# Three more groups convolved as split float32r parts, their row loads moved, and a pass's last products reordered

## The chip, the cores and the metric

The kernel runs on one core of a Trainium2 chip. The core has five engines that run their own instruction streams in order: TensorE (PE, matrix products; its weight loads are listed as PEld), VectorE (DVE), ScalarE (ACT), GpSimd (POOL) and SyncE (SP), which here issues most transfers. The metric is the device time of one execution in microseconds (us); lower is better. The kernel before takes 1276.77 us, the median of three runs (1275.79 to 1277.69).

## The reference

The input x has 8 sequences of 3584 rows of 192 float32 values. A causal convolution with 7 taps, one softmaxed tap vector for each of 8 heads of 24 columns, is followed by a routed two-layer network: each of the 28672 rows goes to the one of 8 experts with the highest gate logit.

```python
w = softmax(weight)                                   # (8 heads, 7 taps)
out = einsum('hk,bskhg->bshg', w, windows of x_pad)   # x -> (28672, 192)
logits = x @ w_gate + modality_bias[modality_id]
e_idx = argmax(logits); gate_w = softmax(logits)[e_idx]
for e in range(8):
    h = maximum(x[mask] @ w1[e], 0.0)                 # 192 -> 1024
    out[mask] = gate_w[mask, None] * (h @ w2[e])      # 1024 -> 192
```

## The kernel before

**Routing.** The rows are taken in 19 groups (`QUADS_OF_GROUP`), of up to 16 tiles of 112 rows; a quad is 4 tiles, 384 KB of x. For a group the kernel loads its quads (`load`), convolves the 8 heads (`convolve`), turns the result (`turn`, DVE transposes), computes gate logits on PE (`gate`), picks the expert (`choose`), computes each row's place in its expert's list (`place`) and scatters rows and gate weight to the DRAM buffer `routed_rows` from POOL (`send`).

**Two ways to convolve.** The groups below `WHOLE_X` multiply the float32 rows (tile `x`) with the float32 matrix `band`, one matmul for each head, which the profile shows as two records. The others first split the rows into a float32r high part `xh` (a cast on ACT, L100) and the rest `xl` (a subtraction on DVE, L101), and add three float32r products: `xh`·`band_hi`, `xl`·`band_hi`, `xh`·`band_lo`. Their quads arrive in a ring of three buffers `xr`, of which the first, `xr_0`, is also the memory of `band`; the first load into it must wait for the last float32 convolution.

**Experts.** Whenever enough rows are routed, a table (`table`) hands out slots: an expert and a number of passes of 256 rows. A slot loads its expert's weights (`Slot.__init__`, into `raw`), gathers its rows from `routed_rows` (`bring`, tiles `near`, `far`, `tags`), splits the weights into float32r parts (`Slot.split`: `w1b`, `w2b`, again a cast on ACT and a subtraction on DVE), and turns the rows of each pass (`turn`: `tp`, `sxh`, `sxl`, `sxs`). A pass has four steps. In a step, `first` makes ten products (L704) of the rows with w1 into `hps`, ACT makes `hh` (relu) and DVE makes `hl` (L708) from it; two steps later `second` multiplies `hh` and `hl` with `w2b` into two PSUM tiles `po`, one for each half of the pass's rows. After a pass's last step `put` scales `po` on ACT (`lowp`) and DVE (`o`, L740), and POOL scatters it to the output.

**Order.** The routing of later groups is cut into parts, and `run` advances as many parts in each step as `due` says, from marks that count the parts of the groups (`parts_of`). ACT keeps the order of the program; on the other engines a scheduler sets it. Every engine then executes its own list in order.

```python
QUADS_OF_GROUP = (1, 1, 2, 2, 2) + (4,) * 14
WHOLE_X = 10
LAG = 2
GROUPS_OF_CHUNK = (5, 2, 2, 2, 2, 2, 2, 2, 0, 0)
SLOTS_OF_CHUNK = (4, 3, 3, 4, 3, 4, 3, 3, 3)
PASSES_OF_SLOT = (2, 4, 4, 4, 4, 4, 4, 4, 2, 1)
```

So the first 4 slots have 2 passes each, 32 steps, during which the rest of groups 5 and 6 and most of group 7 are routed; later slots have 4 passes.

Of the kernel before, what the change touches and what calls it, by code (L numbers as in the profile page):

```python
# [18 lines left out]
P = 128  # L19
MB = 112  # L20
HALO = 16
QUADS_OF_GROUP = (1, 1, 2, 2, 2) + (4,) * 14
WHOLE_X = 10
WHOLE_Y = 5
HEAD_BANKS = dict(turn=1, logit=2, place=2)
ORDERED = {mybir.EngineType.Activation}
# [17 lines left out]
def conv_then_routed_ffn(ctx, tc, x, weight, modality, w_gate, mod_bias, w1, w2, out):  # L44
    nc = tc.nc
    NB, S, D = x.shape
# [8 lines left out]
    NF = FF // P  # L55
    NJ = T // P
# [27 lines left out]
    def ring(pool, n, shape, dtype, name, tag=None):  # L84

        tag = tag or name
        k = turns[tag] = turns.get(tag, -1) + 1
        return pool.tile(shape, dtype, name=name, tag=f"{tag}_{k % n}", bufs=1)
# [135 lines left out]
    class Group:  # L224


        def __init__(self, g, chunk):
            self.chunk, self.xr, self.whole_x, self.whole_y = chunk, [], g < WHOLE_X, g < WHOLE_Y
            self.place_x = ("xh", "xl")[g % 2 if self.whole_x else 0]
# [170 lines left out]
    def parts_of(g):  # L400

        return H + 5 + 3 * QUADS_OF_GROUP[g] + (QUADS_OF_GROUP[g + 1] if WHOLE_X <= g + 1 < NG else 0)

# [7 lines left out]

    def body(cur, after):

        if after:
            for q in range(min(3, after.quads)):
                after.load(q)
        for h in range(H):
            cur.convolve(h)
            yield
        cur.bias_of()  # L420
        gates = []
        ready, step_of = [], 1 if cur.whole_y else 2
        for t in range(cur.quads + 2):
            if t < cur.quads:
                cur.turn(t)
                yield
            if t == 0 and after and after.whole_x and after.quads > 3:
                after.load(3)
            if ready and ready[0][1] < t:
                t0, _, terms = ready.pop(0)  # L430
                gates.append((t0, cur.gate(terms)))
            yield
            if t < cur.quads:
                terms = cur.part_turned(t)
                if (t + 1) % step_of == 0 or t + 1 == cur.quads:
                    ready.append((4 * (t // step_of * step_of), t, terms))
            yield
            while gates:
                cur.logits(*gates.pop(0))
        cur.choose()  # L440
        yield
        if after and not after.whole_x:
            for q in range(after.quads):
                after.part(q)
                if q == 0 and after.quads > 3:
                    after.load(3)
                yield
# [163 lines left out]
    class Slot:  # L611


        def __init__(self, i, chunk, ent):
            self.i, self.h, self.passes, self.rows, self.ends, self.tags = i, {}, plan[chunk][2] // T, {}, {}, {}
            self.chunk, self.ent, load = chunk, ent, nc.sync
            with tc.issue_after(state["load"]) if "load" in state else nullcontext():
                e = load.value_load(ent[:, 1:2], min_val=0, max_val=E - 1)
                new = load.value_load(ent[:, 2:3], min_val=0, max_val=1)
            w1e = w1[bass.ds(e, 1), :, :].rearrange("e p n -> (e p) n")  # L620
            w2e = w2[bass.ds(e, 1), :, :].rearrange("e (c p) d -> p (e c) d", p=P)
            only = dict(cond=new, cond_hint=False)
            load.dma_start(out=raw1[i % 2][:, 0, :], in_=w1e[0:P, :], **only)
            for r in range(2):
                state["load"] = load.dma_start(out=raw1[i % 2][r * DB:(r + 1) * DB, 1, :], in_=w1e[P:D, :], **only).ins

            def load_second():
                state["load"] = load.dma_start(out=raw2[i % 2], in_=w2e, **only).ins

            self.load_second = load_second  # L630
            if i > 0:
                load_second()
# [78 lines left out]
        def second(self, k, fp):  # L711
            wb = w2b[self.i % 2]
            hh, hl = self.h.pop((k, fp))
            if fp == 0:
                self.po = [ring(ps_g2, 2, [P, 2 * D], F32, "po") for _ in range(NJ)]
            for u in range(2):
                c = 2 * fp + u
                for j, po in enumerate(self.po):
                    js = slice(j * P, (j + 1) * P)

                    def by_hi():
                        nc.tensor.matmul(po, hh[:, u, js], wb[:, c, :], start=c == 0, stop=c == NF - 1,  # L722
                                         skip_group_check=True)

                    def by_lo():
                        nc.tensor.matmul(po[:, 0:D], hl[:, u, js], wb[:, c, 0:D], start=False, stop=False,  # L726
                                         skip_group_check=True)

                    for product in (by_lo, by_hi) if c == NF - 1 else (by_hi, by_lo):
                        product()  # L730
            if fp == NF // 2 - 1:
                self.put(self.h.pop(("tag", k)))

# [201 lines left out]
```

## Time and profile before

| | us |
|---|---|
| median of three runs | 1276.77 |
| the profiled execution | 1274.14 |
| its span, first to last instruction | 1272.4 |
| PE busy / PEld busy | 1221.3 / 1187.7 |
| DVE busy | 1001.7 |
| ACT busy | 736.9 |
| POOL busy | 519.2 |

The profiled execution is one run of its own: 1.74 us lie around its span, and it stands 2.63 us below the median. Busy time counts an engine's instructions once where they overlap. A row of a window gives its length, then for each engine the busy time and in brackets the number of instructions, then the TensorE clock that was granted, the share of time in which the DMA engines were busy, and GB/s.

### The profile page before, as it was taken

Reading aid. Unit: us, or ns where it says so; the run is one execution under the profiler, and the core shown is the slowest. Engines: PE = TensorE matmul, PEld = TensorE weight load, DVE = VectorE, ACT = ScalarE, POOL = GpSimd, SP = SyncE. Lnnn points to the kernel's source line nnn. Section 1 sums busy time; section 2 is a strip of 40 time slices with the busy share of each in tenths; the row PEclk is TensorE's granted clock in tenths of the full one; section 3 lists DMA queues with packets and bytes.
Section 4 is the critical chain, followed back from the end, with each engine's and each line's share of the span. In section 5 each row is a group of like instructions: output and inputs, shape, how many; then the busy total and the mean of one; then the engine's idle time right before and its main releaser. Section 6 shows DMA issues by size and latency. Waiting matters only on the chain.

```text
span 1272.4 us, 28546 instructions
## 1 busy us (share of the span) xinstructions
PE 1221.3 (96%) x9106; PEld 1187.7 (93%) x9106; DVE 1001.7 (79%) x2545; ACT 736.9 (58%) x1644; POOL 519.2 (41%) x574
## 2 busy tenths in 40 slices
PE   8559999999999999999999999999999999999996
PEld 6438899999999999999999999999999999999996
DVE  6559988887888778877888788877876676687895
ACT  2226565566666556656665666556555555566774
POOL 5745763625353532624454442613526122121221
PEclk9869999999999999999999999999999999999999
DMA  6567475435453445424355445424424135494440
GB/s 180 158 164 174 125 196 106 108 83 134 100 145 79 98 95 120 133 44 111 63 133 147 110 103 119 114 56 103 101 48 132 37 77 109 104 248 105 91 101 18
DMA packets 314836, 142.24 MB, mean 112 GB/s; under 512 B 229042, under 2 KB 301355, under 8 KB 314676
## 3 DMA queue, kind: packets, MB, share of 16 engines
q1 hardware_dynamic: 289060, 94.97, 35.4%
q0 software_dynamic: 23232, 44.30, 11.0%
q8 instruction: 73, 1.20, 0.4%
q10 hardware_dynamic: 2384, 1.06, 0.3%
q14 instruction: 87, 0.71, 0.2%
HBM read 118.16 MB, written 51.82 MB: 134 GB/s over the span
## 4 chain that ended last, share of the span: by engine, by line
PE 77%; DVE 7%; issue 4%; DMA 4%; POOL 3%; SPq 2%; ACT 2%; DVEq 0%; POOLq 0%; ACTq 0%
PE hps L704 36%; PE po L722 23%; PE po L726 11%; PE cv L276 5%; PE gt L320 3%; POOL routed_rows L212 2%; DVE hl L708 2%; SPq L653 2%; DVE w1b L101 1%; DMA raw<-in_moe_w_dram 1%; DMA routed_rows<-y,idx 1%; DVE w2b L101 1%; DMA near<-routed_rows 1%; ACT lowp L738 0%; DVE sxs L691 0%
## 5 line engine op out<-in xcount | busy, mean ns | idle before, releaser
L722 PE MATMUL po<-w2b,hh 128*128 128x384 f32 x1824 | 556.2, 355 | 3.6 <-DVE o L740 3.4
L704 PE MATMUL hps<-sxh,w1b 128*128 128x256 f32 x1824 | 484.7, 288 | 2.7 <-DVE hl L708 1.3
L741 POOL DMA_INDIRECT out_dram<-o,tags x228 | 233.6, 1024 | 555.8 <-DVE o L740 492.2
L707 ACT ACTIVATE hh<-hps 128x512 fp32r<-128x512 f32 x456 | 273.1, 599 | 314.4 <-PE hps L704 309.1
L708 DVE SCALAR_TENSOR_TENSOR hl<-hps,hh 128x512 fp32r<-128x512 f32 x456 | 311.2, 685 | 178.0 <-ACT hh L707 175.5
L726 PE MATMUL po<-w2b,hl 128*128 128x192 f32 x1824 | 442.6, 253 | 0.0
L704 PE MATMUL hps<-sxs,w1b 128*128 128x256 f32 x1824 | 363.3, 281 | 0.5 <-DVE sxs L691 0.5
L704 PEld LDWEIGHTS hps<-sxh,w1b 128*128 128x128 f32 x1824 | 343.9, 189 | 12.7 <-DVE hl L708 7.9
L722 PEld LDWEIGHTS po<-w2b,hh 128*128 128x128 f32 x1824 | 344.1, 189 | 5.4 <-DVE o L740 4.8
L726 PEld LDWEIGHTS po<-w2b,hl 128*128 128x128 f32 x1824 | 345.7, 190 | 0.0
L212 POOL DMA_INDIRECT routed_rows<-y,idx x256 | 253.7, 991 | 145.4 <-issue 114.2
L704 PEld LDWEIGHTS hps<-sxs,w1b 128*128 128x128 f32 x1824 | 279.6, 189 | 0.9 <-DVE sxs L691 0.7
L704 PE MATMUL hps<-sxl,w1b 128*128 128x256 f32 x912 | 256.1, 281 | 0.6 <-DVE sxl L691 0.6
L704 PEld LDWEIGHTS hps<-sxl,w1b 128*128 128x128 f32 x912 | 172.5, 189 | 3.2 <-DVE sxl L691 0.8
L101 DVE TENSOR_TENSOR w1b<-raw,w1b 128x512 fp32r<-128x512 f32 x152 | 101.1, 675 | 6.6 <-ACT w1b L100 6.1
L738 ACT ACTIVATE lowp<-po,tags 128x192 f32<-128x192 f32 x228 | 83.7, 418 | 31.8 <-PE po L722 31.3
L281 ACT COPY y<-cv 112x192 f32<-112x192 f32 (+1 forms) x198 | 53.4, 319 | 75.5 <-PE cv L276 54.6
L100 ACT CAST w1b<-raw 128x512 fp32r<-128x512 f32 x152 | 92.4, 620 | 0.8
L101 DVE TENSOR_TENSOR w2b<-raw,w2b 128x384 fp32r<-128x384 f32 x152 | 80.9, 542 | 10.3 <-ACT w2b L100 10.0
L740 DVE SCALAR_TENSOR_TENSOR o<-po,tags,lowp 128x192 f32<-128x192 f32 x228 | 84.9, 411 | 4.8 <-ACT lowp L738 2.5
L689 ACT CAST sxs<-tp 64x128 fp32r<-64x128 f32 x228 | 67.9, 298 | 32.6 <-DVE tp L682 29.8
L100 ACT CAST w2b<-raw 128x384 fp32r<-128x384 f32 x152 | 76.1, 512 | 1.0
(133 smaller groups left out, 1032.0 us busy)
## 6 DMA issues: line engine op xcount, KB each, us to landing
raw<-in_moe_w_dram SPq DMA_DIRECT2D x38, 768.0 KB
raw<-in_moe_w_dram SPq DMA_DIRECT2D x38, 512.0 KB
raw<-in_moe_w_dram SPq DMA_DIRECT2D x76, 256.0 KB
xr<-in_x_dram SPq DMA_DIRECT2D x36, 384.0 KB
near<-routed_rows SPq DMA_DIRECT2D x212, 64.0 KB
x<-in_x_dram SPq DMA_DIRECT2D x26, 384.0 KB
far<-routed_rows SPq DMA_DIRECT2D x456, 16.0 KB
routed_rows<-filler SPq DMA_DIRECT2D x8, 776.0 KB
```

The costliest lines, as they stand in the source:

```text
L100: nc.scalar.copy(out=hi, in_=raw)
L101: return nc.vector.tensor_tensor(out=lo, in0=raw, in1=f(hi), op=ALU.subtract).ins
L212: state["scatter"] = nc.gpsimd.indirect_dma_start(out=scr, out_offset=bass.IndirectOffsetOnAxis(ap=idx, axis=0), in_=src, in_offset=None,).ins
L689: nc.scalar.copy(out=hi, in_=raw)
L704: nc.tensor.matmul(hps[:, u, :], wa[:, c, fs], mv[z], start=n == 0, stop=n == len(terms) - 1)
L707: nc.scalar.activation(out=hh, in_=hps, func=AF.Relu)
L708: turn_behind(nc.vector.scalar_tensor_tensor(out=hl, in0=hps, scalar=0.0, in1=f(hh), op0=ALU.max, op1=ALU.subtract))
L722: nc.tensor.matmul(po, hh[:, u, js], wb[:, c, :], start=c == 0, stop=c == NF - 1, skip_group_check=True)
L726: nc.tensor.matmul(po[:, 0:D], hl[:, u, js], wb[:, c, 0:D], start=False, stop=False, skip_group_check=True)
L738: nc.scalar.activation(out=lowp, in_=po[:, D:2 * D], func=AF.Copy, scale=gate)
L740: turn_behind(nc.vector.scalar_tensor_tensor(out=o, in0=po[:, 0:D], scalar=gate, in1=lowp, op0=ALU.mult, op1=ALU.add))
L741: st = nc.gpsimd.indirect_dma_start(out=out, out_offset=bass.IndirectOffsetOnAxis(ap=tag.bitcast(I32)[:, j, 1:2], axis=0), in_=o, in_offse ...
```

## The change

It has four edits. `WHOLE_X` goes from 10 to 7, so groups 7, 8 and 9 are convolved by parts; with it `parts_of` counts four more parts for groups 6, 7 and 8, and `due` asks for them. In `body`, a group that is the first by parts has its first three quads loaded behind the convolution of the group ahead of it, not in front. The weight loads of slots 0 and 1 lose their condition. In `second`, the eight products of a pass's last step, for each half of a `u` pair, are sorted by half: all four of the first `po`, then all four of the second.

```diff
-WHOLE_X = 10
+WHOLE_X = 7
...
     def body(cur, after):
 
-        if after:
+        band_free = after and cur.whole_x and not after.whole_x
+        if after and not band_free:
             for q in range(min(3, after.quads)):
                 after.load(q)
         for h in range(H):
             cur.convolve(h)
             yield
+        if band_free:
+            for q in range(min(3, after.quads)):
+                after.load(q)
         cur.bias_of()
...
-            only = dict(cond=new, cond_hint=False)
+            only = dict(cond=new, cond_hint=False) if i > 1 else {}
...
-            for u in range(2):
-                c = 2 * fp + u
-                for j, po in enumerate(self.po):
-                    js = slice(j * P, (j + 1) * P)
...
+            at = [(u, j) for u in range(2) for j in range(NJ)]
+            if fp == NF // 2 - 1:
+                at = sorted(at, key=lambda uj: uj[1])
+            for u, j in at:
+                c, po = 2 * fp + u, self.po[j]
+                js = slice(j * P, (j + 1) * P)
...
```

What the change moves is seen in the instruction lists; the numbers behind names tell buffers apart, and lines 704, 708, 722, 726 and 740 of before are 708, 712, 728, 732 and 746 of after.

On DVE, before, behind the tenth `hl` stand the end of `choose` for group 6, the two `o` of a pass, and the next pass's `tp`:

```order
L708 SCALAR_TENSOR_TENSOR hl_1516<-hps_1504,hh_1515 128x512
L352 TENSOR_REDUCE first_1554<-rk_1551 112x16
L353 TENSOR_TENSOR oh_1550<-rk_1551,first_1554 112x128
L740 SCALAR_TENSOR_TENSOR o_1529<-po_1348,tags_841,lowp_1527 128x192
L740 SCALAR_TENSOR_TENSOR o_1536<-po_1349,tags_841,lowp_1534 128x192
L355 TENSOR_REDUCE den_1557<-ex_1547 112x16
L680 STREAM_TRANSPOSE tp_1566<-near_1074 128x256
L356 TENSOR_SCALAR den_1557<-den_1557 112x16
L101 TENSOR_TENSOR w1b0_89<-raw1_0_85,w1b0_89 128x512
```

The same place on DVE after the change, around the tenth `hl` and the two `o` of that pass:

```order
L101 TENSOR_TENSOR xl_1480<-xr_1204,xh_1479 128x768
L101 TENSOR_TENSOR w1b0_89<-raw1_0_85,w1b0_89 128x512
L712 SCALAR_TENSOR_TENSOR hl_1546<-hps_1534,hh_1545 128x512
L746 SCALAR_TENSOR_TENSOR o_1559<-po_1371,tags_841,lowp_1557 128x192
L746 SCALAR_TENSOR_TENSOR o_1566<-po_1372,tags_841,lowp_1564 128x192
L101 TENSOR_TENSOR xl_1480<-xr_1206,xh_1479 128x768
L101 TENSOR_TENSOR xl_1480<-xr_1208,xh_1479 128x768
L684 STREAM_TRANSPOSE tp_1579<-near_1070 128x256
L686 STREAM_TRANSPOSE tp_1579<-far_1071 128x128
L101 TENSOR_TENSOR xl_1480<-xr_1483,xh_1479 128x768
```

The four subtractions `xl` of group 7 now stand among these. Between the 4th and the 24th `hl` of the program DVE's list has 177 instructions before and 184 after: eight `xl` more (groups 7 and 8), one `idx` less, and otherwise the same.

On SP, before, three loads of group 7 (`x_968`) stand behind slot 0's second weight load, ahead of all that slot 1 asks for:

```order
L653 ISA
L653 DMA tags_841<-routed_rows 128x4x2
L628 ISA
L628 DMA raw2_0_87<-in_moe_w2_dram 128x8x192
L254 DMA x_968<-in_x_dram 128x4x192 x3
```

After, slot 1's table entry is read there at once, and group 7's loads stand later; its last quad, `xr_1483`, stands inside the gather of slot 3's rows:

```order
L632 DMA raw2_1_88<-in_moe_w2_dram 128x8x192
L643 TENSOR_LOAD tab_798
L643 ISA x2
L657 ISA
L657 DMA near_1516<-routed_rows 32x16x32
L254 DMA xr_1483<-in_x_dram 128x4x192
L657 ISA
L657 DMA near_1516<-routed_rows 32x16x32
```

On PE, before, the last step of a pass takes the two `po` in turn:

```order
L722 MATMUL po_7070<-w2b0_91,hh_7095 128x384
L726 MATMUL po_7070<-w2b0_91,hl_7096 128x192
L722 MATMUL po_7071<-w2b0_91,hh_7095 128x384
L726 MATMUL po_7071<-w2b0_91,hl_7096 128x192
L726 MATMUL po_7070<-w2b0_91,hl_7096 128x192
L722 MATMUL po_7070<-w2b0_91,hh_7095 128x384
L726 MATMUL po_7071<-w2b0_91,hl_7096 128x192
L722 MATMUL po_7071<-w2b0_91,hh_7095 128x384
```

After, it finishes one and then the other (here in another pass):

```order
L708 MATMUL hps_6763<-sxs_6663,w1b1_90 128x256 x2
L728 MATMUL po_6685<-w2b1_764,hh_6712 128x384
L732 MATMUL po_6685<-w2b1_764,hl_6713 128x192 x2
L728 MATMUL po_6685<-w2b1_764,hh_6712 128x384
L728 MATMUL po_6686<-w2b1_764,hh_6712 128x384
L732 MATMUL po_6686<-w2b1_764,hl_6713 128x192 x2
L728 MATMUL po_6686<-w2b1_764,hh_6712 128x384
```

The first `po` is complete four products ahead of the end where it was two ahead. The count and the kinds of products stay as they were.

More of the change, by code (lines that the diff above doesn't have):

```diff
@@ L715, in second, with by_hi, by_lo @@
                 self.po = [ring(ps_g2, 2, [P, 2 * D], F32, "po") for _ in range(NJ)]
-            for u in range(2):
-                c = 2 * fp + u
-                for j, po in enumerate(self.po):
-                    js = slice(j * P, (j + 1) * P)
[L721 to L730, printed above, removed]
+            at = [(u, j) for u in range(2) for j in range(NJ)]
[4 more added lines that the diff above has]
+                js = slice(j * P, (j + 1) * P)
+                def by_hi():
+                    nc.tensor.matmul(po, hh[:, u, js], wb[:, c, :], start=c == 0, stop=c == NF - 1,
+                                     skip_group_check=True)
+                def by_lo():
+                    nc.tensor.matmul(po[:, 0:D], hl[:, u, js], wb[:, c, 0:D], start=False, stop=False,
+                                     skip_group_check=True)
+                for product in (by_lo, by_hi) if c == NF - 1 else (by_hi, by_lo):
+                    product()
             if fp == NF // 2 - 1:
```

## The prediction

> **What bounds the kernel now.** I read the page's shares first, then the busy time by stretch, then the waits of the two busiest engines inside the stretch that the change touches.
>
> ```profile
> span 1272.4 us, 28546 instructions
> PE 1221.3 (96%) x9106; PEld 1187.7 (93%) x9106; DVE 1001.7 (79%) x2545; ACT 736.9 (58%) x1644; POOL 519.2 (41%) x574
> ```
>
> By these shares PE is the bound, and any product that the change saves would be time saved. But the shares are a mean over stages. I cut the span at the end of the 4th and of the 24th `hl` (steps 4 and 24), where the instruction lists begin and cease to differ most:
>
> ```profile
> 100.58 0.65 DVE L708 SCALAR_TENSOR_TENSOR hl<-hps,hh 128x512 fp32r<-128x512 f32 x1
> 168.42 0.68 DVE L708 SCALAR_TENSOR_TENSOR hl<-hps,hh 128x512 fp32r<-128x512 f32 x1
> ...
> 101.20:169.10 67.90, 62.33 (x433) 56.65 (x432) 64.19 (x178) 41.40 (x97) 39.41 (x41) 1.00 0.60 149
> 169.10:265.70 96.60, 96.40 (x710) 92.13 (x709) 79.77 (x200) 57.61 (x131) 51.26 (x56) 1.00 0.54 128
> 265.70:1180.00 914.30, 912.62 (x6993) 908.46 (x6993) 725.62 (x1777) 547.36 (x1198) 350.38 (x375) 1.00 0.46 105
> ```
>
> Behind 169 us PE is busy all the time (96.40 of 96.60) and DVE has a fifth of its time free. In the stretch from 101.2 to 169.1 us it is the other way: DVE is busy for 64.19 of 67.90 us, 94.5%, and PE stands for 5.6. Twenty steps take 67.90 us there, 3.4 each; behind it the next 36 (to the 60th `hl`) take 96.60, 2.7 each. The stretch is slow because weights are split for slots of only two passes while two and a half groups are routed. Who waits for whom in it:
>
> ```profile
> PE po L722 <- DVE o L740: 2.4, 3, 0.9
> PE gt L320 <- DVE gx L101: 1.5, 2, 1.2
> PE gt L320 <- ACT gx L100: 1.2, 1, 1.2
> PE hps L704 <- DVE hl L708: 0.2, 1, 0.2
> ...
> DVE w2b L101 <- ACT w2b L100: 0.9, 2, 0.6
> DVE w1b L101 <- ACT w1b L100: 0.8, 1, 0.8
> DVE hl L708 <- ACT hh L707: 0.6, 2, 0.3
> DVE o L740 <- ACT y L281: 0.2, 1, 0.2
> ```
>
> The upper rows are PE's, the lower DVE's, of this stretch alone. All but one of PE's waits end with a DVE instruction, and that one with the cast that feeds one. DVE's own waits come to 2.5 us and none is for a transfer. So DVE sets the time for twenty steps, and PE sets it from there to the last slots.
>
> [...]
>
> **DVE's added work.** Eight of the twelve new `xl` subtractions, those of groups 7 and 8, stand between the 4th and the 24th `hl` in the new list, and nothing else is added there. Their price:
>
> ```profile
> L101 DVE TENSOR_TENSOR xl<-xr,xh 128x768 fp32r<-128x768 f32 x36 | 33.9, 941 | 0.2
> 115.14 0.95 DVE L101 TENSOR_TENSOR gx<-turned,gx 128x768 fp32r<-128x768 f32 x1
> 116.01 1.02 DVE L101 TENSOR_TENSOR w2b<-raw,w2b 128x384 fp32r<-128x384 f32 x2
> ```
>
> One lasts 941 ns; back to back, the next instruction begins 0.87 us behind an operation of the same shape (115.14 to 116.01). I take 0.87: 8 × 0.87 = 7.0 us. If the added work filled all of DVE's free time in the stretch (67.90 − 64.19 = 3.7), the stretch would grow by 3.3; if the free time stayed, by 7.0. It can grow by more: between the tenth `hl` and the next the new list has three `xl`, 2.6 us more in one interval, and five heads of products follow in one piece on PE with four PSUM buffers, so PE and DVE wait for each other by turns. I allow 2 us for this, the size of PE's waits for `o` above. Between 3.3 and 9.0 I take 6.0: DVE's free time now comes in pieces behind ACT's casts, which do not get shorter, so about 1 us of it can be filled.
>
> [...]
>
> **ACT's added work.** The same eight casts are 0.83 us each, 6.6 us by the row below, on an engine that is busy for 41.40 of 67.90. I cost them at nothing: ACT's free 26.5 us hide them. Where they stand ahead of a relu they delay it by up to 0.83 us; that is in the 2 us above.
>
> ```profile
> L100 ACT CAST xh<-xr x36: 821/832/841, 281.2 to 866.3; 128x768 fp32r<-128x768 f32 x36
> ```
>
> **PE's products.** A float32 head costs 1.29/2 = 0.645 us; one by parts three starts 0.17 us apart, 0.52:
>
> ```profile
> 123.86 1.29 PE cv L276 x4
> ...
> 289.81 0.36 PE L722 MATMUL po<-w2b,hh 128*128 128x384 f32 x1
> 290.00 0.25 PE L726 MATMUL po<-w2b,hl 128*128 128x192 f32 x1
> 290.09 0.36 PE L722 MATMUL po<-w2b,hh 128*128 128x384 f32 x1
> 290.29 0.33 PE L276 MATMUL cv<-xh,band_hi 128*112 128x384 f32 x1
> 290.46 0.33 PE L276 MATMUL cv<-xl,band_hi 128*112 128x384 f32 x1
> 290.63 0.34 PE L276 MATMUL cv<-xh,band_lo 128*112 128x384 f32 x1
> 290.81 0.34 PE L276 MATMUL cv<-xh,band_hi 128*112 128x384 f32 x1
> ```
>
> That saves 0.125 us a head, 3.0 for 24. Eleven of the heads (group 7, three of group 8) lie in the stretch where PE waits anyway and save nothing. The 13 others lie behind it: −1.6 us. Group 9's four `xl` lie there too, beside PE, where DVE has 16.8 us free.
>
> **A pass's end.** The first `po` is complete 0.28 us earlier, one product of 384 columns and one of 192 (289.81 to 290.09 above). PE's waits for `o` are the only ones that this can shorten. The two behind 169 us come to 1.0 us by the row below, so the gain is between 0 and 2 × 0.28; I take −0.4. The three in the stretch are DVE's time and stay.
>
> ```profile
> PE po L722 <- DVE o L740: 1.0, 2, 0.8
> ```
>
> The order of products itself (one pair more of two narrow ones in a row, one of two wide) changes no count; I cost it at nothing, between −0.3 and +0.3 us over 57 passes, which is 5 ns each, the size of the spread of PE's starts above.
>
> **The loads.** Three loads of 384 KB leave SP ahead of slot 1, whose gather was then slow:
>
> ```profile
> 83.80 2.17 SPq L254 DMA_DIRECT2D x<-in_x_dram  x3
> 90.92 7.70 SPq L653 DMA_DIRECT2D near<-routed_rows  x4
> 108.78 1.96 SPq L653 DMA_DIRECT2D near<-routed_rows  x4
> 121.57 5.16 SPq L653 DMA_DIRECT2D near<-routed_rows  x4
> ...
> 106.26 0.73 DVE L740 SCALAR_TENSOR_TENSOR o<-po,tags,lowp 128x192 f32<-128x192 f32 x2
> 106.91 0.43 DVE L680 STREAM_TRANSPOSE tp<-near 128x256 f32<-128x256 f32 x1
> ```
>
> Slot 1's gather can come up to 2.2 + 5.7 us earlier. But the transpose that first needs it, at 106.91 us, follows on `o` at once, without idle time ahead of it: DVE is late, not the rows. I take 0, from −1 to +0.5. The new load of `xr_1483` must wait on SP for the first `xl` of group 7, and slot 3's gather is queued behind it until about 128 us; that gather stood at 121.57 before, and the transposes that need it stand ahead of the 23rd `hl`, near 165 us, so it is covered. The lost conditions of slots 0 and 1 leave a few register instructions on SP's way: 0. POOL's scatters are the same in number, and POOL is busy for 39.41 of the 67.90 us.
>
> **Sum.** +6.0 − 1.6 − 0.4 + 0 + 0 = +4.0 us. Against the profiled execution's own 1274.14 (span 1272.4) that is 1278.1; against the median of the runs, 2.63 us higher, 1276.77 + 4.0 = 1280.8. The ends of the terms give −0.2 (3.3 − 1.6 − 0.6 − 0.3 − 1.0) and +8.2 (9.0 − 1.6 − 0 + 0.3 + 0.5).
>
> **Rivals.**
> - *DVE fills its gaps.* The new splits stand where DVE waited for ACT, the stretch grows by 3.3 only, and 3.3 − 1.6 − 0.4 = +1.3: 1278.1, which is no change that can be told. For it speaks that 3.7 us are free and DVE's work is all there is; against it that 2.5 us of them are waits for ACT, which gets more work itself. It decides if DVE's free time falls under 2 us.
> - *PE sets the stretch after all: faster.* If PE's 62.33 busy us were its need, all 24 heads would save, −3.0 − 0.4 = 1273.4, with nothing for DVE. It would need DVE's extra 7.0 us to fit into 3.7 free ones, or slot 1's earlier rows to shift the whole stretch by more than 3.3 us; the waits above speak against the first, the missing idle time at 106.91 against the second. [...]
> - *Late rows.* The last quad of group 7 is asked for only when its first is split, and ACT, which runs in program order, stands with the relus behind its cast. Of 36 such casts one waited before, 0.5 us, but in the stretch DMA is busier (0.60 against 0.46). Two waits of 2 us on ACT, for groups 7 and 8, would add 4: 1284.8.
>
> ```profile
> ACT xh L100 <- DMA xr<-in_x_dram: 0.5, 1, 0.5
> ```
>
> **How the numbers follow.** The forecast (1279.4 to 1284) gets 0.55, the gaps filled 0.20, faster 0.13, late rows 0.12. The range leaves out most of "faster" and the upper part of "late rows": 1276.3 to 1285. A measurement of this kernel tells about 0.2%, 2.55 us, from no change: slower 0.55 + 0.12 = 0.67, same 0.20, faster 0.13.
>
> **What would show it.** Right: the 4th to the 24th `hl` lie about 74 us apart, with DVE at 95% or more; from there to the 60th about 95 us, with PE at 99%; the `xl` count is 48; the gather of slot 1 is quick and moves nothing. Wrong: the stretch is no longer than 70 us, or the 4th `hl` ends several us ahead of 101 us (then transfers counted ahead of it), or ACT waits for `xr` by microseconds.

## The result and the profile after

The changed kernel takes 1293.35 us (median of 4 runs, 1293.05 to 1297.33) against 1276.28 us (1275.33 to 1277.69) for the kernel before on the same chip. The ratio is 1.014 with a 95% interval of 1.0118 to 1.0162. Slower was forecast, but +4.0 us; it was +17.1, and 1293 lies outside the range. The profiled execution took 1293.05 us. One sign that the prediction named as speaking against it is there: ACT waits for `xr` by microseconds.

Of the kernels below, ring4, poolq, whole10 and cond ran where the kernel before takes 1276 us, all later ones where it takes 1519 to 1524 us and engines stand still again and again for nothing that the trace shows (last section), so each is read against the kernel before, or a neighbour, of its own session and mostly by stretch.

The shares of the page after the change:

```profile
span 1291.3 us, 28601 instructions
PE 1225.2 (95%) x9130; PEld 1198.1 (93%) x9130; DVE 1007.0 (78%) x2557; ACT 754.9 (58%) x1656; POOL 517.8 (40%) x574
```

They have hardly moved. Where the time went shows only by stretch. I cut at the same steps as before, from the end of the 4th `hl` (now 103.5 us) to the 12th (137.5), the 24th (187.2) and the 60th (286.2). The columns are the length of the stretch, the busy time of PE, PEld, DVE, ACT and POOL, the granted clock, the DMA share and GB/s:

```profile
103.50:137.50 34.00, 26.14 (x180) 25.14 (x179) 30.63 (x72) 20.81 (x46) 16.70 (x20) 0.95 0.60 140
137.50:187.20 49.70, 38.16 (x272) 36.83 (x271) 39.97 (x117) 27.28 (x61) 19.49 (x21) 0.93 0.49 135
187.20:286.20 99.00, 96.92 (x724) 95.82 (x723) 81.78 (x204) 60.58 (x133) 52.77 (x56) 0.98 0.52 121
```

The 4th to the 12th step before, in a window 0.2 us wider:

```profile
101.00:128.00 27.00, 24.13 (x169) 22.00 (x169) 25.50 (x59) 17.07 (x38) 12.68 (x15) 1.00 0.67 154
```

With the ends of the same `hl` before (101.2, 128.0, 169.1, 265.7) the spans differ so: start +2.3, 4th to 12th +7.2 (34.0 against 26.8), 12th to 24th +8.5 (49.6 against 41.1), 24th to 60th +2.5, the rest −1.6; together +18.9, the difference of the two spans. DVE is busy for 30.63 + 39.97 = 70.6 us from the 4th to the 24th step, 6.4 more than before, as counted. But the stretch grew by 15.7, and DVE's share of it fell from 94.5% to 84%. Something else is waited for. The waits of that stretch, from the answer on who waits for whom (total us, times, longest):

```profile
ACT xh L100 <- DMA xr<-in_x_dram: 14.8, 2, 8.7
...
PE cv L276 <- ACT xh L100: 8.8, 1, 8.8
...
DVE xl L101 <- ACT xh L100: 7.7, 2, 7.2
...
PE hps L708 <- DVE hl L712: 4.4, 1, 4.4
...
DVE ad L374 <- PE rp L371: 1.7, 1, 1.7
```

There are two troubles. The first is a chain from a transfer: ACT waits 14.8 us in two pieces for `xr`, and PE, through ACT's cast, 8.8 us in one. The second has no transfer in it: PE waits 4.4 us for an `hl`, and ahead of that DVE waits for PE's `rp`.

**The late rows.** SP's own waits from 120 to 180 us:

```profile
SPq L622 <- DVE past L573: 25.9, 1, 25.9
SPq L254 <- DVE xl L101: 5.5, 1, 5.5
```

Its issues behind them in the timeline (start, us):

```profile
164.77 0.36 SPq L627 DMA_DIRECT2D raw<-in_moe_w_dram  x1
165.49 1.26 SPq L629 DMA_DIRECT2D raw<-in_moe_w_dram  x2
167.09 0.39 SPq L632 DMA_DIRECT2D raw<-in_moe_w_dram  x1
168.56 0.34 SPq L657 DMA_DIRECT2D near<-routed_rows  x1
169.00 0.62 SPq L254 DMA_DIRECT2D xr<-in_x_dram  x1
```

And the cast on ACT that waits for the last of them, in ACT's timeline:

```profile
176.77 0.83 ACT L100 CAST xh<-xr 128x768 fp32r<-128x768 f32 x1 [8.65 <-DMA xr<-in_x_dram]
```

SP runs its list in order: it stood for 25.9 us at line 622, where it reads slot 4's row of the table (`past` is part of the table), and the load of group 8's last quad came behind that, behind slot 4's weights (1792 KB by the sizes that the page gives for these issues) and the first piece of a gather. It was issued at 169.00, when ACT had been waiting for it for 0.9 us, and took 7.75 us with those weights asked for just ahead of it. PE stood from 168.5, when its last product ahead of the hole began, to 177.7. Group 7's last quad is the other wait (6.15 us on ACT, until 131.75); it falls mostly inside the trouble that follows.

**The bunch.** DVE's list around the 9th and the 10th `hl` (the 9th is at 121.22):

```profile
122.89 0.29 DVE L353 TENSOR_TENSOR oh<-rk,first 112x128 bf16<-112x128 f32 x1
123.09 0.20 DVE L358 RECIPROCAL y<-den 112x8 f32<-112x8 f32 x1
125.01 0.28 DVE L374 COPY ad<-rp 112x120 f32<-112x120 f32 x1 [1.72 <-PE rp L371]
...
126.90 0.17 DVE L387 CAST idx<-row 112x16 int32<-112x16 f32 x1
126.99 0.95 DVE L101 TENSOR_TENSOR xl<-xr,xh 128x768 fp32r<-128x768 f32 x1
127.86 0.74 DVE L101 TENSOR_TENSOR w1b<-raw,w1b 128x512 fp32r<-128x512 f32 x1
128.53 0.68 DVE L712 SCALAR_TENSOR_TENSOR hl<-hps,hh 128x512 fp32r<-128x512 f32 x1
```

Before, the end of `choose` for group 6 (`oh`) stood behind the 10th `hl` and `place` (`ad`, the scan, ... `idx`) behind the 12th, and DVE did not wait for `rp`:

```profile
121.37 0.29 DVE L353 TENSOR_TENSOR oh<-rk,first 112x128 bf16<-112x128 f32 x1
...
127.31 0.68 DVE L708 SCALAR_TENSOR_TENSOR hl<-hps,hh 128x512 fp32r<-128x512 f32 x1
127.91 0.27 DVE L374 COPY ad<-rp 112x120 f32<-112x120 f32 x1
```

Now both stand behind the 9th. `place` needs `rp`, which PE makes from `oh` behind the products that it has in its own list; DVE waits 1.72 us, then does seven small operations (`ad` among them), an `xl` and a `w1b`, and the 10th `hl` follows 3.5 us behind the wait's end. PE begins `rp`'s product at 124.76 and the next product only at 129.35. The second row of the waits, 5.5 us for an `xl` on SP, is the load of group 7's last quad: its buffer comes free only with the `xl` at 126.99.

**The clock behind an idle PE.** Both holes are followed by products at a lower clock (last but two columns):

```profile
124.00:128.00 4.00, 0.97 (x10) 0.83 (x8) 2.82 (x9) 1.59 (x3) 0.12 (x1) 1.00 0.17 34
128.00:132.00 4.00, 2.65 (x10) 2.68 (x11) 4.00 (x8) 0.25 (x1) 3.09 (x4) 0.66 0.70 173
...
176.00:180.00 4.00, 2.34 (x9) 2.29 (x10) 2.37 (x5) 2.36 (x5) 0.00 (x0) 0.50 0.32 39
180.00:184.00 4.00, 4.00 (x30) 3.98 (x29) 2.72 (x9) 3.20 (x10) 1.98 (x2) 0.94 0.80 211
```

An estimate from these rows, busy time by (1 − clock): 0.9 us behind the first hole, 1.2 + 0.2 behind the second. The first is too low, since its row's clock is also a mean over 1.35 us in which PE still stood: from 129.4 to 132.6 us alone the clock is 0.50 and PE busy throughout, which makes 1.6. By this estimate each of the two holes cost about one and a half us more than itself. It counts half of the busy time at 0.50 as lost; by PE's timeline two products of `po` (384 and 192 columns) then take 0.53 us from start to start (129.70 to 130.23), and 0.29 at 1.00 (134.90 to 135.19), so the estimate is a little high.

### The profile page after: what moved, and what is told of

Same layout as the page of the kernel before. It is cut to its first block, busy times and chain, and to the rows that moved or that the text cites. A ratio compares the mean times of both kernels' runs of the same rounds, so it can differ in the third digit from the quotient of the medians.

```text
span 1291.3 us, 28601 instructions
## 1 busy us (share of the span) xinstructions
PE 1225.2 (95%) x9130; PEld 1198.1 (93%) x9130; DVE 1007.0 (78%) x2557; ACT 754.9 (58%) x1656; POOL 517.8 (40%) x574
## 4 chain that ended last, share of the span: by engine, by line
PE 75%; DVE 6%; issue 3%; DMA 3%; POOL 2%; ACT 2%; SPq 1%; DVEq 0%; POOLq 0%; ACTq 0%
PE hps L708 36%; PE po L728 22%; PE po L732 11%; PE cv L276 4%; PE gt L320 2%; DVE hl L712 1%; DMA routed_rows<-y,idx 1%; POOL routed_rows L212 1%; DVE w1b L101 1%; ACT hh L711 1%; DMA near<-routed_rows 1%; DMA xr<-in_x_dram 1%; DMA out_dram<-o,tags 1%; DVE o L746 1%; DVE w2b L101 0%
## 5 line engine op out<-in xcount | busy, mean ns | idle before, releaser
L747 POOL DMA_INDIRECT out_dram<-o,tags x228 | 236.2, 1036 | 568.2 <-DVE o L746 512.4
L712 DVE SCALAR_TENSOR_TENSOR hl<-hps,hh 128x512 fp32r<-128x512 f32 x456 | 311.4, 685 | 177.7 <-ACT hh L711 175.0
L732 PE MATMUL po<-w2b,hl 128*128 128x192 f32 x1824 | 427.4, 255 | 0.0
L728 PEld LDWEIGHTS po<-w2b,hh 128*128 128x128 f32 x1824 | 336.7, 190 | 5.7 <-DVE o L746 5.3
L708 PEld LDWEIGHTS hps<-sxl,w1b 128*128 128x128 f32 x912 | 173.6, 190 | 0.1
L744 ACT ACTIVATE lowp<-po,tags 128x192 f32<-128x192 f32 x228 | 96.0, 422 | 19.0 <-PE po L728 11.4
L101 DVE TENSOR_TENSOR w1b<-raw,w1b 128x512 fp32r<-128x512 f32 x152 | 101.2, 676 | 6.2 <-ACT w1b L100 6.2
L746 DVE SCALAR_TENSOR_TENSOR o<-po,tags,lowp 128x192 f32<-128x192 f32 x228 | 88.2, 411 | 9.7 <-DMA out_dram<-o,tags 7.5
```

Of the source, the lines that this page charges most:

```text
L101: return nc.vector.tensor_tensor(out=lo, in0=raw, in1=f(hi), op=ALU.subtract).ins
L708: nc.tensor.matmul(hps[:, u, :], wa[:, c, fs], mv[z], start=n == 0, stop=n == len(terms) - 1)
L712: turn_behind(nc.vector.scalar_tensor_tensor(out=hl, in0=hps, scalar=0.0, in1=f(hh), op0=ALU.max, op1=ALU.subtract))
L744: nc.scalar.activation(out=lowp, in_=po[:, D:2 * D], func=AF.Copy, scale=gate)
L746: turn_behind(nc.vector.scalar_tensor_tensor(out=o, in0=po[:, 0:D], scalar=gate, in1=lowp, op0=ALU.mult, op1=ALU.add))
L747: st = nc.gpsimd.indirect_dma_start(out=out, out_offset=bass.IndirectOffsetOnAxis(ap=tag.bitcast(I32)[:, j, 1:2], axis=0), in_=o, in_offse ...
```

## The experiments

The theories. *Late rows*: the loads of the last quads, held up on SP, account for most of the 17 us. *Work*: DVE's eight added subtractions do. A third came from the trace above, *bunch*: `place` standing next to `choose` on DVE, and the hole and clock behind it. In the recorded expectations these have other names too: Theory 1 is late rows, Theory 2 and D are work, B is the bunch, and P is the pace at which routing is advanced, which the count of parts sets. (In whole10 and cond the theories are about the other edits and the late start.) First the transfers.

**Four buffers, all quads asked for together (ring4).** To make room, `lg` and `bt` have one buffer:

```diff
-... else ring(xp, 3, [P, 4, D], F32, "xr")
+... else ring(xp, 4, [P, 4, D], F32, "xr")
-            for q in range(min(3, after.quads)):
+            for q in range(after.quads):
-                if q == 0 and after.quads > 3:
-                    after.load(3)
```

> The changed kernel with a fourth buffer in the ring of row loads, so that a group's last quad is asked for with the other three and waits for no split (two small routing tiles are single-buffered to make the room). Theory 1, late rows: the two waits of ACT for a last quad (6.1 and 8.7 us in the changed kernel) and what follows from them make up most of the loss, so the stretch from the 4th to the 24th hl falls from 81 to about 68 to 72 us and the time to 1278 to 1282. Theory 2, split work on a full DVE: the waits only stood where DVE would have been late anyway; the time stays at 1288 or more.

Measured: 1281.79 us (1279.62 to 1284.17, 5 runs) against 1276.15, ratio 1.0039 [1.0026, 1.0052]. ACT has no wait for `xr` left, so by the medians some 11.5 of the 17 us are gone. That is not the price of the late rows alone. The profiled run, the slowest of the five (1284.17), is 8.9 us shorter in its span than the changed kernel's: 6.8 lie between the 12th and the 24th `hl` (42.8 against 49.6), where group 8's row was late; 2.4 in the start; 2.4 between the 24th and the 60th, where DVE in the changed kernel waits 5.3 us for output scatters, in ring4 2.6; and the 4th to the 12th took 2.9 us longer (36.9). So the time is in the range of Theory 1, but the stretch from the 4th to the 24th `hl` is not: it takes 79.7 us, where 68 to 72 were expected. The longest of those waits of the changed kernel:

```profile
DVE o L746 <- DMA out_dram<-o,tags: 3.7, 1, 3.7
```

In ring4 the bunch is as it was, now without a transfer. Its waits from the 4th to the 24th `hl`:

```profile
PE hps L706 <- DVE hl L710: 4.4, 1, 4.4
...
DVE ad L374 <- PE rp L371: 2.4, 1, 2.4
```

And its busy times and clock in pieces of 4 us:

```profile
116.00:120.00 4.00, 4.00 (x20) 4.00 (x20) 2.88 (x8) 0.19 (x1) 0.89 (x2) 0.50 0.91 243
120.00:124.00 4.00, 4.00 (x29) 4.00 (x29) 2.08 (x10) 3.14 (x7) 0.10 (x1) 0.90 1.06 255
124.00:128.00 4.00, 1.15 (x11) 1.00 (x9) 2.65 (x8) 3.01 (x5) 0.00 (x0) 0.96 0.44 57
128.00:132.00 4.00, 2.47 (x9) 2.50 (x10) 4.00 (x8) 0.00 (x0) 3.05 (x3) 0.50 0.47 78
132.00:136.00 4.00, 4.00 (x22) 3.61 (x21) 3.65 (x11) 2.32 (x8) 3.31 (x3) 0.69 0.94 285
```

By these rows the clock alone costs 2.0 + 0.4 + 1.2 + 1.2 = 4.8 us (an estimate, as above) beside a hole of 4.6 us between the starts of two products. Together that is the size of most of the 10.1 us by which the eight steps are longer than before; how far the two add up is not shown, and 2.4 of the 4.8 come ahead of the hole.

**The last quads through POOL's queue (poolq).**

```diff
-                nc.sync.dma_start(out=xr, ...)
+                queue = nc.gpsimd if self.late and q == 3 else nc.sync
+                queue.dma_start(out=xr, ...)
```

> The changed kernel, with the last quad of groups 7 and 8 alone asked for from POOL's queue in place of SP's; three buffers as in the changed kernel. Theory 1, late rows behind SP's wait for a table: group 8's last quad no longer stands behind slot 4's table and weights, so at least the 8.7 us wait goes and the time is 1279 to 1285; group 7's wait (its buffer comes free late) may stay. Theory 2: 1288 or more. If the wait for the buffer, not SP's queue, made the rows late, also 1288 or more.

Measured: 1303.05 us, ratio 1.0215 [1.0202, 1.0229], slower still. ACT's wait for the rows:

```profile
ACT xh L100 <- DMA xr<-in_x_dram: 24.3, 2, 17.4
```

POOL runs in order too, and in its timeline the load stands among the scatters of a routed group:

```profile
135.81 0.93 POOL L212 DMA_INDIRECT routed_rows<-y,idx  x1 [0.30 <-issue]
137.05 0.93 POOL L212 DMA_INDIRECT routed_rows<-y,idx  x1 [0.30 <-issue]
137.98 0.84 POOL L256 DMA_DIRECT2D xr<-in_x_dram  x1
```

The transfer itself took 4.06 us. So the load's place in a list makes it late, and the time follows the lateness: 24.3 us of waits on ACT, 96.3 us from the 4th to the 24th `hl`. The way round SP was a wrong cure: 1279 to 1285 us were expected of it.

**All but the parts of groups 7 to 9 (whole10).**

```diff
-WHOLE_X = 7
+WHOLE_X = 10
```

> The changed kernel with groups 7 to 9 convolved in float32 again; the lost condition of slots 0 and 1, the order of a pass's last products and the place of the first loads by parts (now group 10's) stay. Theory 1: these three edits are worth 0 to -1 us, so 1275.3 to 1276.5. Rival: the start (2.3 us later in the changed kernel) or the pass's end costs by itself; then 1278 to 1281.

Measured: 1277.35 us, ratio 1.0014 [1.0005, 1.0022]. The other edits together cost 1.2 us by the medians and 1.8 by the ratio, where −0.4 was forecast, and the conversion of the groups nearly all of the 17; the time lies between the two ranges expected. In one session the medians are 1276.15 for before, 1277.35 for whole10 and 1281.79 for ring4: of the 17 us some 1.2 belong to the other edits, 4.4 to what ring4 still has (work, bunch and products together), and 11.6 are what the fourth buffer takes away. What whole10 loses, it loses mostly in the start: the 4th `hl` ends at 103.3, as in the changed kernel. ACT's timeline of before shows slot 0's four weight casts in one piece:

```profile
76.20 2.43 ACT L100 CAST w1b<-raw 128x512 fp32r<-128x512 f32 x4
84.77 0.31 ACT L346 ACTIVATE ex<-ex 112x128 f32<-112x128 f32 x1 [6.14 <-DVE ex L345]
```

The changed kernel's does not:

```profile
76.13 1.15 ACT L100 CAST w1b<-raw 128x512 fp32r<-128x512 f32 x2
83.01 0.31 ACT L346 ACTIVATE ex<-ex 112x128 f32<-112x128 f32 x1 [5.73 <-DVE ex L345]
83.23 1.12 ACT L100 CAST w1b<-raw 128x512 fp32r<-128x512 f32 x2
```

Two of them now stand in ACT's list behind an `ex` that waits for DVE, 7 us later. Whether that makes the start late, the next run tells.

**The conditions back (cond).**

```diff
-            only = dict(cond=new, cond_hint=False) if i > 1 else {}
+            only = dict(cond=new, cond_hint=False)
```

> The changed kernel with the condition of the weight loads of slots 0 and 1 put back. Theory A, the 2.3 us by which the 4th hl came later are due to the order in which slot 0's weights and rows are asked for on SP: about 2 us are regained, 1291. Theory B, they come from elsewhere in the scheduler's list or from the TensorE clock being lower by chance there: no change, 1293.

Measured: 1288.82 us, ratio 1.0104 [1.0085, 1.0122], some 4.5 us under the changed kernel, more than either theory gave it. But not by the start: its 4th `hl` ends at 104.3, although the four casts stand together again, so the split casts are not what makes the start late. Most of the gain lies in the 4th to the 12th step (31.3 us against 34.0), where in its list `place` stands behind the 10th `hl` and `oh` behind the 9th. Whether the conditions themselves cost anything stays open; ring4, which lacks them too, starts as early as the kernel before (101.1). What the three late starts share is a low clock: from 90 to 95 us, around the first `hl`, 0.50 was granted in the changed kernel, whole10 and cond, 0.65 in ring4 and 1.00 before. That was not tried apart.

**Work and bunch apart.** Eight subtractions of the same shape put on DVE in the kernel before (dve8, where `lg` and `bt` have one buffer as in ring4), the eight `xl` taken out of ring4 (ring4_noxl: the low parts of groups 7 and 8 are left out, and PE multiplies the high part by `band_lo` in their place), the count of parts put back in ring4 (ring4_pace), and the count alone put into the kernel before, with empty parts (pace):

```diff
 dve8, from before
+        if after and after.g in (7, 8):
+            for q in range(4):
+                idle = ring(xp, 1, [P, 4, D], F32, "idle")
+                nc.vector.tensor_tensor(out=idle, in0=after.x[:, 4*q:4*q+4, :], in1=after.x[:, 4*q:4*q+4, :], op=ALU.subtract)
 ring4_noxl, from ring4
-            split(self.xh[:, part, :], self.xl[:, part, :], self.xr[q])
+            if self.no_low:
+                nc.scalar.copy(out=self.xh[:, part, :], in_=self.xr[q])
+            else:
+                split(self.xh[:, part, :], self.xl[:, part, :], self.xr[q])
 ring4_pace, from ring4 (in parts_of)
-(QUADS_OF_GROUP[g + 1] if WHOLE_X <= g + 1 < NG else 0)
+(QUADS_OF_GROUP[g + 1] if 10 <= g + 1 < NG else 0)
 pace, from before (in parts_of; and four bare yields a group in body)
-(QUADS_OF_GROUP[g + 1] if WHOLE_X <= g + 1 < NG else 0)
+(QUADS_OF_GROUP[g + 1] if 7 <= g + 1 < NG else 0)
```

> The kernel before with eight more DVE subtractions of 128x768 float32 on rows already there, four behind the choice of experts of group 6 and four behind group 7's, into a buffer that nothing reads; no change on PE, ACT or in the loads. Theory D, DVE sets the stretch: 7.0 us more work between the 4th and the 24th hl cost 3.3 to 7.0 us, 1279.5 to 1283. Theory B, the loss comes from where waits fall in the order, not from the amount of work on DVE: 0 to 2 us, 1276 to 1278.

> The kernel with the fourth row buffer, without the eight DVE subtractions of groups 7 and 8: their low part is left out, and PE multiplies the high part in its place, so PE, ACT and the loads keep their work. Theory D, the rest of the loss is DVE's added work: the time falls by 4 to 6 us, 1276 to 1278. Theory B, the rest is the place behind the choice around the ninth hl and PE's wait for it, which stays: it falls by 0 to 2 us, 1280 to 1282.

> The kernel with the fourth row buffer (1281.8), its marks counting the parts of groups as before, so that routing is advanced less densely; group 8's splits then stand behind the 24th hl, and the place of group 6 no longer directly behind its choice. Theory B, what is left of the loss is the bunch around the tenth hl, for which PE waits 4.4 us: 1276 to 1279. Theory D: the work on DVE is the same in all, four splits only move behind the full stretch; it gains half of the DVE term, 1279 to 1280.5.

> The kernel before with four empty parts each behind groups 6, 7 and 8 and with these counted in the marks, as the change counts them; no work is added. It sets the pace at which routing is advanced as in the changed kernel. Theory P, the denser pace bunches routing in the full stretch: 2 to 4 us slower, 1278 to 1280. Theories D and B: within 1 us, 1275 to 1277.5.

Measured: dve8 1.0019 [1.0004, 1.0033], ring4_noxl 1.0039 [1.0023, 1.0054], ring4_pace 1.0166 [1.015, 1.0181], pace 0.9995 [0.9983, 1.0008]. These fell into the first of the 1520 us sessions, and the whole time of ring4_pace, 25 us over before, is what no theory gave. So three were run again, with ring4 beside them:

> The kernel before with eight subtractions of 128x3072 bytes a partition (0.87 to 0.96 us each) put on VectorE where the changed kernel splits groups 7 and 8; nothing else is changed, group 6's choosing and placing stay apart (behind the 10th and the 12th hl). Work theory (eight more operations on the busiest engine of the stretch make it longer by about their time): 1281 to 1284, ratio 1.004 to 1.006. Bunch theory (what is left of the loss with four buffers is VectorE waiting in its order for a TensorE result, and the halved clock behind it): at most 1.5 us over before, ratio up to 1.0012.

> The changed kernel with four buffers for the quads, without the low parts of groups 7 and 8 (the eight xl on VectorE are left out; TensorE multiplies the high part instead, as many products as before): choosing and placing of group 6 still stand together behind the 9th hl. Work theory: the loss is gone, 1275 to 1277.5, ratio 0.999 to 1.001. Bunch theory: the bunch costs what it did but for the one xl in it, TensorE idle 3.5 us between the 9th and the 10th hl, 1279.5 to 1282, ratio 1.003 to 1.0045.

> The changed kernel with four buffers for the quads, and the count of parts that paces groups 6 to 8 as in the kernel before: all eight xl are still made, but group 6's choosing stands behind the 10th hl and its placing behind the 13th, instead of both behind the 9th. Bunch theory: no TensorE idle of 4 us between the 9th and the 14th hl, no halved clock behind it, 1276 to 1279, ratio 1.000 to 1.002. Work theory: as ring4, 1281 to 1283, ratio 1.004 to 1.005.

> The changed kernel with four buffers for the quads, beside the three others on one chip. Both theories: as the first time, ratio 1.003 to 1.005; VectorE's placing of group 6 behind the 9th hl waits 2.4 us for rp, TensorE idles 4.6 us.

Measured: dve8_again 1.0012 [0.9998, 1.0026], r4_noxl_again 1.0039 [1.0025, 1.0054], r4_pace_again 1.0176 [1.0154, 1.0198], ring4_again 1.0063 [1.0043, 1.0082]. By these ratios work alone costs 1.8 to 2.9 us of 1522, the order without the work 5.9. Two things limit the first figure. Of dve8's eight subtractions only six stand between the 4th and the 24th `hl`; two stand ahead of the 4th. And DVE is busy for 78 to 80% of that stretch in these sessions, not for 94.5%, so it has gaps to fill that it lacks at 1276 us. By the stretch alone the six cost more: it takes 86.1, 86.1 and 88.0 us in the three runs of dve8, against 83.0 and 83.4 in half (below) and 81.0 in pace. ring4_pace missed again by 27 us. Its lists from the 4th to the 24th `hl` are what was wanted, but for four `xl` that now stand behind the 24th, and its times there are about those of half. The busy times from the 4th to the 12th step, first of ring4_again:

```profile
126.40:160.70 34.30, 27.54 (x172) 26.50 (x173) 31.12 (x74) 19.75 (x42) 10.81 (x12) 0.87 0.63 156
```

Of r4_noxl_again:

```profile
126.30:164.60 38.30, 31.62 (x183) 30.61 (x184) 27.89 (x71) 20.26 (x42) 11.61 (x14) 0.79 0.59 144
```

Of r4_pace_again:

```profile
124.50:152.10 27.60, 24.17 (x168) 22.60 (x168) 26.91 (x61) 18.59 (x38) 5.77 (x6) 0.96 0.60 127
```

Of dve8_again:

```profile
123.70:151.20 27.50, 24.58 (x163) 22.57 (x163) 26.90 (x61) 16.88 (x38) 5.38 (x6) 0.94 0.57 127
```

Of half (below):

```profile
122.30:148.90 26.60, 24.14 (x163) 21.79 (x163) 25.24 (x59) 16.98 (x38) 5.45 (x6) 0.98 0.58 130
```

The two with the bunch have a low clock (0.87 and 0.79, against 0.94 to 0.98) and 34 to 38 us, with or without `xl`; those without it have 27, with two added subtractions or none. The table has, for each kernel, the `hl` behind which `oh` and the scan of group 6's `place` stand on DVE, DVE's wait for `rp`, the longest gap between the starts of two products on PE from the 4th to the 12th `hl`, the added subtractions in that stretch, and the stretches by the ends of the `hl` (poolq is left out, since its late row of 17.4 us falls into the first):

| kernel | `oh`, `place` | wait for `rp`, us | longest gap on PE, us | added | 4th–12th, us | 12th–24th, us |
|---|---|---|---|---|---|---|
| before | 10, 12 | 0 | 1.5 | 0 | 26.8 | 41.1 |
| whole10 | 10, 11 | 0 | 1.4 | 0 | 31.3 | 37.6 |
| cond | 9, 10 | 0 | 2.8 | 4 | 31.3 | 48.6 |
| after | 9, 9 | 1.7 | 4.6 | 4 | 34.0 | 49.6 |
| ring4 | 9, 9 | 2.4 | 4.6 | 4 | 36.9 | 42.8 |
| half | 10, 12 | 0 | 1.5 | 0 | 26.6 | 56.5 |
| pace | 9, 12 | 0 | 2.9 | 0 | 27.7 | 53.4 |
| dve8_again | 10, 12 | 0 | 1.5 | 2 | 27.4 | 58.7 |
| r4_pace_again | 10, 13 | 0 | 1.6 | 2 | 27.6 | 55.5 |
| r4_pace_w9 | 10, 11 | 0 | 2.1 | 0 | 32.0 | 52.7 |
| ring4_again | 9, 9 | 1.7 | 4.6 | 4 | 34.3 | 55.2 |
| r4_noxl_again | 9, 9 | 2.5 | 3.7 | 0 | 38.4 | 53.2 |
| ring4_noxl | 9, 9 | 2.5 | 3.7 | 0 | 39.5 | 51.4 |

Two or three steps between `choose` and `place` give 27 us, one gives 31 to 32, none 34 to 40. These are two effects. With one step or more DVE does not wait for `rp` at all. The 4 us between 27 and 31 are mostly a matter of where the stretch is cut: in the kernels of 27 us `place` and what hangs on it come behind the 12th `hl` (in before `ad` starts at 127.91, the 12th `hl` ends at 127.99), in the others ahead of it, and whole10, 4.5 us longer than before in the first stretch, is 3.5 shorter in the second (r4_pace_w9 against half of its session: 5.4 and 3.8). With no step DVE waits 1.7 to 2.5 us, PE stands for 3.7 to 4.6, and the clock falls behind that; this is the bunch, and it stays when the eight `xl` are taken out (the two noxl rows). The added work does not decide the first column of times (cond with four `xl` has 31.3 us like whole10 with none), but it is not free either: two subtractions come with 27.4 to 28.1 us in dve8 and the r4_pace kernels, none with 26.6 to 27.7.

From the 4th to the 24th step the cut does not matter: r4_pace_again takes 83.1 us, like half (83.0) and pace (81.0), against 86.1 for dve8_again, 89.5 for ring4_again and 91.5 for r4_noxl_again. It loses its 27 us between the 60th and the 400th `hl` (1064.9 us against 1038 to 1045 for the other kernels of the sessions).

**For the usual clock, and for a better version.** These also fell on 1520 us:

> As r4_pace_again: four buffers for the quads and the old pacing of groups 6 to 8, all eight xl made. On a chip where the kernel before takes about 1276 us. Bunch theory: 1276 to 1279.5, ratio 1.000 to 1.0025. Work theory: 1281 to 1283.5, ratio 1.004 to 1.006.

> As dve8_again: the kernel before with eight subtractions on VectorE and nothing else. On a chip where the kernel before takes about 1276 us. Bunch theory: at most 1.5 us over it, ratio up to 1.0012. Work theory: 5 to 7 us, ratio 1.004 to 1.006.

> The kernel before with only the last products of a pass taken half by half. Both theories: the step of the prediction gave it -0.4 us, so ratio 0.999 to 1.0005; if it is what makes the kernel with ten whole groups slower than before, 1.001 to 1.002.

> A version that could beat both: four buffers for the quads, the old pacing, and only group 9 convolved by parts beyond the kernel before, whose work falls where TensorE sets the pace; the other edits as in the change. Bunch theory: 1274.5 to 1277.5, ratio 0.9985 to 1.0005. Work theory: four xl more where VectorE has room, the same.

> As r4_pace_3, for a chip where the kernel before takes about 1276 us. Bunch theory: 1276 to 1279.5, ratio 1.000 to 1.0025. Work theory: 1281 to 1283.5, ratio 1.004 to 1.006. Where engines wait for nothing the trace shows and the kernel before takes 1520 us: 1.013 to 1.018 again, most of it between the 60th and the 400th hl.

> As half: the kernel before with only the last products of a pass taken half by half, -0.4 us or ratio 0.9995 by the prediction's step; 0.9975 to 0.9999 was measured where the kernel before takes 1519 us, and if that carries over, 1273 to 1276.

Measured: r4_pace_3 1.0129 [1.0109, 1.0149] and r4_pace_4 1.0192 [1.0169, 1.0215], once more most or all of it behind the 60th `hl` (their 4th to 24th step 82.1 and 83.1 us); dve8_3 1.0014 [1.0003, 1.0024]. half, the kernel before with only the products' order of a pass's last step changed, gave 0.9987 [0.9975, 0.9999] and 0.9997 [0.9983, 1.0011]: no gain that two runs agree on. r4_pace_w9 (ring4_pace with `WHOLE_X = 9`) gave 1.0041 [1.0027, 1.0056], with `place` one step behind `choose`, 32.0 us, and also 5 to 6 us more behind the 60th than dve8_3 and half of its session. No version beats the kernel before.

What stays open: the whole time of ring4_pace where the kernel before takes 1276 us, why the late sessions punish it far behind the change, and how ring4's last 4 to 6 us divide between work and bunch at 1276 us, since both were taken apart at 1520 us only.

## Why the prediction was wrong

The direction was right, but partly by luck: the term that made it slower, DVE's added work, is the smaller part of what happened. Two steps failed, the loads put at 0 and the waits "by turns" put at 2 us.

- *What bounds the kernel.* DVE's 94.5% was read rightly, but "DVE sets the time for twenty steps" did not mean that the time follows DVE's work. Most of the loss (7.2 + 8.5 of 18.9 us) lies in these steps, and there PE and ACT wait for transfers and for answers, which a busy share does not show. The share itself did not reach 95%, as was to be seen; it fell to 84%, over 83.6 us where 74 were forecast.
- *The loads, 0.* This step failed most. "Covered" was said of slot 3's gather behind the load of group 7's last quad, and nothing of the load itself, nor of group 8's, which stands on SP behind a read of the table and 1792 KB of weights. The rival "late rows" had the right engine and the right mechanism, at 2 us a wait; they were 6.15 and 8.65 us, and its 0.12 and +4 were both too low. Without these waits (ring4) the 12th to the 24th `hl` take 6.8 us less and the whole kernel 11.6 us less, other waits among them.
- *The 2 us "by turns".* Here lies the bunch, between the 9th and the 10th `hl` where I had looked behind the tenth. I counted the `xl` that follow and did not see that `place` had moved up to `choose`, so that DVE now waits for PE in the middle of its own list. The lists showed it; only the trace could price it, and 2 us was taken from waits of another kind. Measured were 1.7 us of waiting on DVE, a hole of 4.6 us on PE and a lower clock behind it. The stretch grew by 7.2 us here and 10.1 in ring4, of which up to 4.5 are `place` standing ahead of the cut and not behind it, as whole10 shows.
- *The clock.* No term had it. By the estimates above the holes cost 1.6 and 1.4 us more than themselves in the changed kernel, and the low clock 4.8 in ring4.
- *DVE's added work, +6.0.* The count and the price were right (6.4 us more busy time; 942 ns an `xl`). Work alone measured +1.8 to +2.9 us (0.0012 to 0.0019 of 1522), with six of the eight in the stretch and DVE less full than at 1276 us; the stretch itself grew by 3 to 5 us. At 1276 us no run has the work alone: ring4 takes 4.4 us more than whole10, and work, bunch and the gain of its products are in that together. So 6.0 is probably too big, and that is not shown. The rival "DVE fills its gaps", with 3.3, lies nearer to what was measured.
- *The conditions and the start, 0.* The start came 2.3 us later. Kernels with and without the conditions, and with the casts of slot 0 together and apart, had the late start, so its cause is not settled; the low clock from 90 to 95 us goes with it in each.
- *The heads and the pass's end, −2.0.* From the 60th `hl` to the end the changed kernel is 1.6 us shorter and ring4 1.8, so a gain of this size is there, but behind the place where the heads were expected to give it; half alone shows no difference that both its runs agree on. From the 24th to the 60th, where 95 us were forecast, ring4 has 96.7 and before 96.6.

## What to carry to other kernels

When a change moves work in in-order lists, look first for operations that wait for another engine's answer (`ad` for `rp`) and have moved up directly behind the operation that asks for it: here that cost DVE 1.7 to 2.5 us and PE a hole of 3.7 to 4.6, and one step between question and answer was enough to make the wait go. Compare stretches only between cuts that have the same work inside. Follow every added load on its queue back to what stands ahead of it, reads of a table included, and price it at the full hold. And where slow products follow a hole on PE, price it at its length plus theirs (by the estimate above 1.6 and 1.4 us behind the holes of 4.6 and 9 us).

## What the hardware showed that was not expected

Two gaps between the starts of PE's products, 2.37 and 1.00 us long, follow on each other in ring4 (from 111.73) and in the changed kernel (from 114.15). They were followed by a granted clock of 0.50 from 116 to 120 us in ring4 and of 1.00 there in the changed kernel. So a short hole was followed by half the clock in one kernel and not in the other, while the holes of 4.6 and 9 us were each followed by half the clock. In ring4 the clock changes at about 114.0, 120.8, 127.6 and 134.5 us, in steps of 6.8 to 6.9 us, and it fell at 114.0 when PE had stood for 2.0 us. In the changed kernel 0.50 was granted from 129.3 to 132.7 us and from 173.6 to 180.5, that is for 3.4 and 6.8 us, and the clock fell when PE had stood for 4.3 and 4.8 us. How long PE had stood when the clock fell thus differs from hole to hole; what decides it is not shown.

In the sessions of 1520 us PE waits again and again for nothing that the profile shows (from 300 to 1100 us of half):

```profile
PE hps L704 <- issue: 38.8, 30, 2.4
PE po L724 <- issue: 38.7, 25, 6.6
PE po L728 <- issue: 18.6, 18, 2.3
```

Of its 148 gaps over 0.5 us between the starts of products, counted in the trace from 90 us on, 21 last between 2.05 and 2.16 us. In the profiled run of before at 1274 us there are 10, 10.1 us together. The same chip gave 1276 us in one session and 1522 in another. What the engines wait for there was not tried. The stretches that are slow differ from kernel to kernel. In half the 240th to the 260th step take 50.5 us, as in before, and the next 20 take 69.1 against 51.4; from the 340th step on it keeps the time of before. r4_pace_again is quick from the 140th to the 160th step (51.1 us), where half is slow (69.3), and slow from the 240th to the 260th (70.7), where half is quick. So its loss of 27 us may come of where these slow stretches fall; no run shows what is left of it at 1276 us.
